# A convolution, a router and a grouped MLP on one core: the band matrix by predicated copies, zero matmuls ahead of the convolution, half batches fetched on two queues, logits in one group

## The chip, the cores and the metric

The kernel runs on one core of a Trainium2 chip. The metric is the time of one execution on the device in microseconds. One further execution was profiled; its trace gives the start and the length of every instruction, what it waited for, and the packets of the DMA engines.

## The reference

`x` is [8, 3584, 192]. A causal convolution of seven taps runs along the sequence, with softmaxed taps for each of eight heads of 24 columns; a linear router gives each of the 28,672 resulting rows to one of eight experts with a capacity of 3,584 each, best score first; each expert is an MLP 192 → 1024 → 192.

```python
w = exp(weight - max); w = w / (sum(w) + 1e-9)            # [8 heads, 7 taps]
out = einsum('hk,bskhg->bshg', w, windows of x, 7 long)   # "attn", [28672, 192]
logits = attn @ w_gate                                    # [28672, 8]
# all (token, expert) pairs in falling order of logit: a token takes the expert
# if it has none yet and the expert holds fewer than 3584
out[mask_e] = relu(attn[mask_e] @ w1[e]) @ w2[e]
```

## The kernel before

**Half batches.** The sequence is worked off in 16 half batches of 1,792 rows. Half batch i is tile X(i), [118, 16, 192] in f32: 16 windows of 112 rows on partitions 6 to 117, and the six rows ahead of each window (the halo) on partitions 0 to 5. Four such tiles take turns. X(i) comes by three transfers, halo, windows 0 to 7 ("first half") and windows 8 to 15 ("second half"). SyncE's queue (SP) issues the first two, ScalarE's queue (ACT) the third; of X(0) SP issues all. The halo of an even half batch has one window of zeros, which GpSimd (POOL) writes.

**Convolution.** `conv(i)` runs one f32 matmul for each head h against TH[:, h], a banded matrix of 118 rows that holds the seven taps on diagonals (`cv<-X,TH`; a trace shows two instructions for an f32 matmul, so 16 for a half batch). ScalarE copies the eight results into tile `a`, then issues the store of `a` to `attn` in DRAM. Four PSUM banks let TensorE run four heads ahead of these copies. Between heads `mid(h)` is called, which puts other work into the same stream.

**Band matrix.** `toeplitz` softmaxes the taps (`wb`) on VectorE and ScalarE, then builds TH head by head out of seven masks MK of 112 columns: VectorE does six heads, ScalarE and GpSimd two.

**Logits.** For half batch i-1 VectorE transposes `a` in 32x32 blocks (`aT`, four instructions), for half batch i-2 TensorE multiplies by the gate matrix `GF` (named `c_mu` in the trace; `pl<-aT,c_mu`, 24 matmuls of 32 output rows in f32, 48 instructions), ScalarE evacuates them, and one transpose (`pt`) puts them into the table LT. The list `left` in `moe_kernel` holds these pieces and `mid` takes one for each head.

**Routing and MLP.** From half batch 6 on, steps of the router (`bg` matmuls, `m_x`, `sl`, `oa`) are mixed in by a planner (`Pace`, `Meter`, `Steps.hook`) that adds up estimated engine times while the program is written, and takes no time at run time. After half batch 15 the MLP follows (`ph`, `hh`, `hl`, `y`), 56 tiles of 512 rows, with gathers and scatters by GpSimd.

**Transfers and their counters.** The built program gives all transfers of SP and ACT eight completion counters in turn (DMAHW0 to DMAHW7). A transfer that takes a counter waits until the transfer that had it before has landed, on the engine that issues it. An engine's instructions start in order, so what stands behind such a wait on ScalarE, the copies out of PSUM too, waits as well.

Of the kernel before, what the change touches and what calls it, by code (L numbers as in the profile page):

```python
# [28 lines left out]
class Meter:  # L29
# [5 lines left out]
    def __getattr__(self, op):  # L35
# [4 lines left out]
        def call(*a, **k):  # L40
# [4 lines left out]
            if self.name == "pe":  # L45
# [3 lines left out]
                p.pe += max(d + 0.0025, 0.027 if bf else 0.107)  # L49
# [64 lines left out]
def build(ctx, tc, nc, x, weight, wg, attn, LT, wk):  # L114
# [10 lines left out]
    pmi = cst.tile([128, 128], I32, name="pmi")  # L125
    P.iota(pmi, pattern=[[-1, 128]], base=0, channel_multiplier=1)
# [3 lines left out]
    P.memset(TH[:, :, W:128], 0.0)  # L130
    MK = cst.tile([128, 7, W], BF, name="MK")
    for j in range(7):
        V.tensor_scalar(MK[:, j], D0[:, 0:W], float(j), None, op0=OP.is_equal)
    wm = cst.tile([128, 8], F32, name="wm")

    def toeplitz():
# [3 lines left out]
        load(1)  # L140
# [4 lines left out]

        tk = cst.tile([128, 2, W], F32, name="tk")
        for h in (1, 5):
            A.activation(TH[:, h, 0:W], MK[:, 0], AF.Copy, scale=wb[:, h, 0:1])
            for j in range(1, 7):
                A.activation(tk[:, j % 2], MK[:, j], AF.Copy, scale=wb[:, h, j:j + 1])  # L150
                P.tensor_tensor(TH[:, h, 0:W], TH[:, h, 0:W], tk[:, j % 2], op=OP.add)
        for hs in ((0, 2), (3, 4), (6, 7)):
            for j in range(7):
                for h in hs:
                    t = TH[:, h, 0:W]
                    if j == 0:
                        V.tensor_scalar(t, MK[:, 0], wb[:, h, 0:1], None, op0=OP.mult)
                    else:
                        V.scalar_tensor_tensor(t, MK[:, j], wb[:, h, j:j + 1], t, op0=OP.mult, op1=OP.add)


    wgr = cst.tile([128, 6, 8], F32, name="wgr")
    GF = wk.tile([128, 6, 32], F32, name="c_mu")
    pm = wk.tile([128, 1], F32, name="pm")

    def gate_ops():
        for pb in range(4):
            nc.sync.dma_start(wgr[32 * pb:32 * pb + 32], wg.rearrange("(c f) e -> f c e", f=32))
        P.memset(GF, 0.0)
        for pb in range(4):  # L170
            q = slice(32 * pb, 32 * pb + 32)
            P.tensor_copy(GF[q, :, 8 * pb:8 * pb + 8], wgr[q])

        pi = cst.tile([128, 1], I32, name="pi")
        P.iota(pi, pattern=[[0, 1]], base=0, channel_multiplier=1)
        V.tensor_scalar(pi, pi, 24, None, op0=OP.bitwise_and)
        V.tensor_scalar(pm, pi, 24.0, -1.0, op0=OP.is_equal, op1=OP.mult)
# [4 lines left out]
    def load(i):  # L182
        t = X[i] = k.xp[i % 4].tile([118, 16, D], F32, name="X")
        b, hf = divmod(i, 2)
        o = x.offset + (b * 3584 + hf * 1792) * D
        if hf == 0:
            P.memset(t[0:6, 0], 0.0)
            nc.sync.dma_start(t[0:6, 1:16], bass.AP(tensor=x.tensor, offset=o + (W - 6) * D,
                                                    ap=[[D, 6], [W * D, 15], [1, D]]))
        else:  # L190
            nc.sync.dma_start(t[0:6], bass.AP(tensor=x.tensor, offset=o - 6 * D, ap=[[D, 6], [W * D, 16], [1, D]]))
        for eng, w in ((nc.sync, 0), (A if i else nc.sync, 8)):
# [46 lines left out]
    k.toeplitz, k.gate_ops = toeplitz, gate_ops  # L239
# [1180 lines left out]
def moe_kernel(ctx, tc, x, weight, wg, w1, w2, out):  # L1420
# [6 lines left out]
    with ExitStack() as cw:  # L1427
# [57 lines left out]
        def tail():  # L1485

            for i in (14, 15):
                for u in range(3):
                    gate(i, u)
                    yield PEA if u == 2 else None  # L1490
                end(i)
# [43 lines left out]
        def gate(i, u):  # L1535
            for f in range(2 * u, 2 * u + 2):
# [11 lines left out]

        k.load(0)
        k.toeplitz()  # L1550
        k.gate_ops()
        k.load(2)
        r.consts()
        for i in range(NHB):
            if i + 3 < NHB:
# [106 lines left out]
```

## Time and profile before

| | |
|---|---|
| median of three runs (lowest, highest) | 1268.86 us (1267.01, 1270.75) |
| the profiled execution: time, span of its instructions | 1268.0 us, 1266.2 us |
| TensorE, VectorE, ScalarE, GpSimd busy | 1222.0, 999.6, 551.2, 510.1 us |
| packets of the DMA engines | 193.02 MB |

The span runs from the first instruction to the last. The 1.8 us between it and the time of the same execution lie outside what the trace shows. Busy time of TensorE counts pipelined matmuls from issue to end, so that rows of matmuls overlap.

### The profile page before, as it was taken

Reading aid. Unit: us, or ns where it says so; the run is one execution under the profiler, and the core shown is the slowest. Engines: PE = TensorE matmul, PEld = TensorE weight load, DVE = VectorE, ACT = ScalarE, POOL = GpSimd, SP = SyncE. Lnnn points to the kernel's source line nnn. Section 1 sums busy time; section 2 is a strip of 40 time slices with the busy share of each in tenths; the row PEclk is TensorE's granted clock in tenths of the full one; section 3 lists DMA queues with packets and bytes.
Section 4 is the critical chain, followed back from the end, with each engine's and each line's share of the span. In section 5 each row is a group of like instructions: output and inputs, shape, how many; then the busy total and the mean of one; then the engine's idle time right before and its main releaser. Section 6 shows DMA issues by size and latency. Waiting matters only on the chain.

```text
span 1266.2 us, 21792 instructions
## 1 busy us (share of the span) xinstructions
PE 1222.0 (97%) x7839; PEld 1049.9 (83%) x7839; DVE 999.6 (79%) x2245; ACT 551.2 (44%) x1220; POOL 510.1 (40%) x504
## 2 busy tenths in 40 slices
PE   5889979999999999999999999999999999999997
PEld 2445558899889888887889999999999999999997
DVE  7398669999999989988857777777777777777772
ACT  4544645565544543643433333333333333333332
POOL 3000435364444443533244444444444444444422
PEclk9999989999999999999999999999999999999999
DMA  9999897999533343423653513242314132231100
GB/s 236 347 334 297 271 328 257 294 316 319 194 103 112 122 152 94 152 93 125 161 126 105 205 41 100 94 155 62 129 48 147 46 102 97 85 105 47 45 26 28
DMA packets 100579, 193.02 MB, mean 152 GB/s; under 512 B 19232, under 2 KB 64752, under 8 KB 96240
## 3 DMA queue, kind: packets, MB, share of 16 engines
q1 hardware_dynamic: 57856, 115.15, 28.1%
q0 software_dynamic: 21504, 44.07, 11.7%
q10 hardware_dynamic: 21104, 32.34, 7.8%
q8 instruction: 63, 1.03, 0.3%
q14 instruction: 52, 0.43, 0.1%
HBM read 116.02 MB, written 75.50 MB: 151 GB/s over the span
## 4 chain that ended last, share of the span: by engine, by line
PE 83%; DVE 7%; DMA 5%; issue 1%; POOL 1%; ACT 1%; SPq 1%; POOLq 0%; ACTq 0%; DVEq 0%
PE ph L55 38%; PE y L55 37%; PE cv L55 3%; PE bg L55 3%; DMA X<-in_x_dram 1%; PE px L55 1%; DVE X L55 1%; DMA raw<-in_moe_w_dram 1%; DVE hl L55 1%; DVE oa L55 1%; DVE aT L55 1%; DMA wgr<-in_moe_w_gate_dram 1%; PE pl L55 1%; DMA X<-otab 1%; POOL xg L1262 0%
## 5 line engine op out<-in xcount | busy, mean ns | idle before, releaser
L55 PE MATMUL y<-w,hh 128*128 128x384 f32 x1792 | 539.3, 356 | 0.0
L55 ACT ACTIVATE hh<-ph 128x512 fp32r<-128x512 f32 x448 | 268.1, 598 | 494.2 <-PE ph L55 493.9
L55 PE MATMUL y<-w,hl 128*128 128x192 f32 x1792 | 448.9, 251 | 0.0
L55 DVE SCALAR_TENSOR_TENSOR hl<-ph,hh 128x512 fp32r<-128x512 f32 x448 | 308.1, 688 | 140.6 <-ACT hh L55 136.6
L55 PE MATMUL ph<-xa,w 128*128 128x512 f32 x1344 | 395.7, 402 | 3.9 <-DVE hl L55 3.9
L55 PEld LDWEIGHTS y<-w,hl 128*128 128x128 f32 x1792 | 341.0, 190 | 15.1
L55 PEld LDWEIGHTS y<-w,hh 128*128 128x128 f32 x1792 | 336.4, 188 | 19.1 <-issue 2.3
L1337 POOL DMA_INDIRECT out_dram<-yo,ib x128 | 127.9, 999 | 288.4 <-DVE yo L55 278.6
L55 PEld LDWEIGHTS ph<-xa,w 128*128 128x128 f32 x1344 | 218.7, 189 | 24.6 <-DVE hl L55 5.2
L1337 POOL DMA_INDIRECT out_dram<-yo,ia x96 | 112.2, 1168 | 262.3 <-DVE yo L55 230.0
L55 DVE STREAM_TRANSPOSE xs<-xg 32x256 f32<-32x256 f32 x496 | 182.9, 369 | 8.5
L55 PE MATMUL ph<-xd,w 128*128 128x512 f32 x448 | 177.3, 396 | 1.5 <-DVE xd L55 1.5
L55 PE MATMUL ph<-xd,dl 128*128 128x512 f32 x448 | 174.5, 390 | 0.0
L1262 POOL DMA_INDIRECT xg<-attn,jb x128 | 137.8, 1076 | 40.9 <-issue 40.9
L1262 POOL DMA_INDIRECT xg<-attn,ja x96 | 110.2, 1147 | 32.1 <-issue 26.7
L55 ACT ACTIVATE yt<-y 128x192 f32<-128x192 f32 x224 | 73.6, 328 | 102.6 <-PE y L55 99.5
L55 PE MATMUL cv<-X,TH 118*128 118x384 f32 x256 | 99.6, 515 | 18.9 <-DVE TH L55 12.5
L55 DVE TENSOR_TENSOR yo<-y,yt 128x192 f32<-128x192 f32 x224 | 79.4, 354 | 40.8 <-ACT yt L55 38.1
L55 PEld LDWEIGHTS ph<-xd,w 128*128 128x128 f32 x448 | 84.2, 188 | 21.2 <-DVE xd L55 2.0
L55 PEld LDWEIGHTS ph<-xd,dl 128*128 128x128 f32 x448 | 84.3, 188 | 19.7
L55 PEld LDWEIGHTS cv<-X,TH 118*128 118x128 f32 x256 | 44.6, 194 | 51.8 <-issue 13.0
L55 ACT ACTIVATE a<-cv 128x384 f32<-128x384 f32 x128 | 59.7, 492 | 53.3 <-PE cv L55 32.0
(237 smaller groups left out, 900.4 us busy)
## 6 DMA issues: line engine op xcount, KB each, us to landing
w<-kw SPq DMA_DIRECT2D x16, 1536.0 KB
w<-kv SPq DMA_DIRECT2D x16, 1536.0 KB
attn<-a ACTq DMA_DIRECT2D x16, 1344.0 KB
kw<-w SPq DMA_DIRECT2D x48, 256.0 KB
kv<-w SPq DMA_DIRECT2D x32, 384.0 KB
X<-in_x_dram SPq DMA_DIRECT2D x17, 672.0 KB
X<-in_x_dram ACTq DMA_DIRECT2D x15, 672.0 KB
raw<-in_moe_w_dram SPq DMA_DIRECT2D x32, 192.0 KB
```

The source lines that it names most:

```text
L55: return f(*a, **k)
L1262: self.nc.gpsimd.indirect_dma_start(out=t[:, b], out_offset=None, in_=self.attn[0:rows], in_offset=bass.IndirectOffsetOnAxis(ap=idx[b], ax ...
L1337: st = self.nc.gpsimd.indirect_dma_start(out=self.out, out_offset=bass.IndirectOffsetOnAxis(ap=idx, axis=0), in_=o, in_offset=None, bounds ...
```

## The change

- TH comes from a narrow band C of 38 columns: a mask MK of [128, 7, 38] compared at once, seven predicated copies that write one tap each for all eight heads, and four copies of 32 partitions into TH, two on VectorE and two on ScalarE.
- 28 bf16 matmuls of a zero tile run ahead of the first convolution (`warm`).
- The gate matrix is fetched once, not four times, and VectorE places it.
- `prep` separates the zeros of the halo from `load`; `load` issues its first part (halo and first half) on SP and its second part on ACT, separately. X(0) is split over both queues too. The second half of X(i+3) is issued behind head 3 of half batch i, no longer ahead of head 0.
- The 24 logit matmuls of a half batch stand together behind head 3.
- The planner's estimate for matmuls with 32 output rows goes down.

```diff
-    D0 = cst.tile([128, 128], BF, name="D0")
-    V.tensor_copy(D0, pmi)
...
+    zb = cst.tile([128, 512], BF, name="zb")
+    V.memset(zb, 0.0)
+    BW = 38
+    pmi = cst.tile([128, 7, BW], I32, name="pmi")
+    P.iota(pmi, pattern=[[-1, 7], [-1, BW]], base=6, channel_multiplier=1)
...
+    V.tensor_scalar(MK, pmi, pf, None, op0=OP.is_equal)
...
+    def warm(n):
+        ps = k.bank("pt")
+        for _ in range(n):
+            PE.matmul(ps, zb[:, 0:128], zb, start=True, stop=True)
...
-        for h in (1, 5):
-            A.activation(TH[:, h, 0:W], MK[:, 0], AF.Copy, scale=wb[:, h, 0:1])
...
+        for j in range(7):
+            V.copy_predicated(C, MK[:, j, None, :].to_broadcast([128, 8, BW]), wb[:, :, j, None].to_broadcast([128, 8, BW]))
+        for a in (0, 3, 1, 2):
+            lo = 32 * a - 6
+            c0, c1 = max(lo, 0), min(32 * a + 32, W)
+            o, i = TH[32 * a:32 * a + 32, :, c0:c1], C[32 * a:32 * a + 32, :, c0 - lo:c1 - lo]
+            if a % 3:
+                V.tensor_copy(o, i)
+            else:
+                A.activation(o, i, AF.Copy)
...
-        for eng, w in ((nc.sync, 0), (A if i else nc.sync, 8)):
+        for p in parts:
+            eng, w = ((nc.sync, 0), (A, 8))[p]
...
-        def gate(i, u):
-            for f in range(2 * u, 2 * u + 2):
+        def gate(i):
+            for f in range(6):
                 k.logits(i, f)
...
+        k.warm(28)
+        for i in range(4):
+            k.prep(i)
         k.load(0)
+        k.load(1)
+        k.gate_load()
+        k.load(2, (0,))
+        k.load(3, (0,))
         k.toeplitz()
+        k.load(2, (1,))
         k.gate_ops()
-        k.load(2)
...
             def mid(h):
+                if h == (3 if i else 7) and i < NHB - 3:
+                    k.load(i + 3, (1,))
...
-                            left.append(partial(gate, i - 2, u) if u < 3 else partial(end, i - 2))
+                            left.append((lambda: None) if u % 2 == 0 else partial(gate if u == 1 else end, i - 2))
```

ScalarE's stream from the first convolution's end to the third's start, before. X_180, X_188, X_278, X_312 and X_352 are X(0) to X(4); a_316, a_357 and a_392 are the results of half batches 0, 1 and 2; `[waits ...]` names the counters and engines waited for.

```order
L193 DMA X_278<-in_x_dram 112x8x192
L193 DMA X_312<-in_x_dram 112x8x192 [waits DMAHW4_49]
...
L204 DMA attn_62<-a_316 112x4x768 [waits DMAHW7_49,Activation_49]
L193 DMA X_352<-in_x_dram 112x8x192 [waits DMAHW3_49,DMAHW2_49,DMAHW1_49]
L55 ACTIVATE a_357<-cv_358 128x16x24 [waits PE_49]
...
L204 DMA attn_62<-a_357 112x4x768 [waits DMAHW5_49,Activation_49]
L193 DMA X_388<-in_x_dram 112x8x192 [waits DMAHW7_49,DMAHW6_49]
L55 ACTIVATE a_392<-cv_393 128x16x24 [waits PE_49]
```

The same engine now, from its first instruction to half batch 2. X_211, X_213, X_214, X_216, X_320 and X_356 are X(0) to X(5); a_283, a_324 and a_359 belong to half batches 0, 1 and 2.

```order
L208 DMA X_211<-in_x_dram 112x8x192
L208 DMA X_213<-in_x_dram 112x8x192
L55 ACT_TABLE_LOAD
...
L208 DMA X_214<-in_x_dram 112x8x192 [waits DMAHW0_49]
...
L208 DMA X_216<-in_x_dram 112x8x192 [waits DMAHW3_49]
L55 ACTIVATE a_283<-cv_315 128x16x24 [waits PE_49]
L219 DMA attn_62<-a_283 112x4x768 [waits DMAHW5_49,Activation_49]
...
L208 DMA X_320<-in_x_dram 112x8x192 [waits DMAHW2_49,DMAHW4_49,DMAHW0_49,Pool_49]
L55 ACTIVATE a_324<-cv_338 128x16x24 [waits PE_49]
...
L55 ACTIVATE a_359<-cv_368 128x16x24 [waits PE_49]
L208 DMA X_356<-in_x_dram 112x8x192 [waits DMAHW6_49,DMAHW5_49]
```

The second halves of X(0) and X(1) now stand ahead of everything on ScalarE, those of X(4) and X(5) between copies inside half batches 1 and 2. DMAHW0 is held by the second half of X(2) when X(4) asks for it, and DMAHW5 by the store of half batch 0 when X(5) asks for it.

SP's first rows, before (X_180, X_188 and X_278 as above):

```order
L188 DMA X_180<-in_x_dram 6x15x192
L193 DMA X_180<-in_x_dram 112x8x192 x2
L191 DMA X_188<-in_x_dram 6x16x192
L193 DMA X_188<-in_x_dram 112x8x192
L168 DMA wgr_141<-in_moe_w_gate_dram 32x6x8 [waits DMAHW0_49]
...
L168 DMA wgr_141<-in_moe_w_gate_dram 32x6x8 [waits DMAHW3_49]
L188 DMA X_278<-in_x_dram 6x15x192 [waits DMAHW5_49]
```

And now:

```order
L202 DMA X_211<-in_x_dram 6x15x192
L208 DMA X_211<-in_x_dram 112x8x192
L205 DMA X_213<-in_x_dram 6x16x192
L208 DMA X_213<-in_x_dram 112x8x192
L176 DMA wgr_143<-in_moe_w_gate_dram 32x6x8
L202 DMA X_214<-in_x_dram 6x15x192 [waits DMAHW1_49]
L208 DMA X_214<-in_x_dram 112x8x192 [waits DMAHW2_49]
```

X(2) now waits for small or early transfers, where it waited behind the four gate transfers and for X(1).

TensorE in half batches 3 and 4, before (`pt` ends the half batch two earlier; counts are matmuls):

```order
L55 MATMUL pt<-ident,L 128x128
L55 MATMUL cv<-X,TH 128x384 x2
L55 MATMUL pl<-aT,c_mu 32x128 x8
L55 MATMUL cv<-X,TH 128x384 x2
L55 MATMUL pl<-aT,c_mu 32x128 x8
L55 MATMUL cv<-X,TH 128x384 x2
L55 MATMUL pl<-aT,c_mu 32x128 x8
L55 MATMUL cv<-X,TH 128x384 x2
L55 MATMUL pt<-ident,L 128x128
```

And now:

```order
L55 MATMUL pt<-ident,L 128x128
L55 MATMUL cv<-X,TH 128x384 x4
L55 MATMUL pl<-aT,c_mu 32x128 x24
L55 MATMUL cv<-X,TH 128x384 x4
L55 MATMUL pt<-ident,L 128x128
```

The matmuls are the same; three groups of logits between heads became one.

## Rows read from the trace of the kernel before

**Rows 1.** Stretches: length, busy (count) per engine, TensorE's granted clock, DMA share, GB/s.

```profile
0.00:10.00 10.00, 0.00 (x0) 0.00 (x0) 6.24 (x25) 4.65 (x12) 3.41 (x14) 1.00 0.75 171
10.00:20.00 10.00, 7.48 (x15) 3.78 (x16) 9.08 (x33) 4.92 (x12) 4.78 (x11) 1.00 1.13 231
...
27.00:33.00 6.00, 4.16 (x40) 2.11 (x40) 2.78 (x4) 0.00 (x0) 0.00 (x0) 1.00 1.05 373
...
45.00:62.50 17.50, 17.50 (x153) 9.24 (x152) 7.86 (x10) 9.96 (x27) 0.25 (x1) 1.00 1.05 337
...
70.00:100.00 30.00, 26.61 (x224) 13.74 (x222) 25.99 (x67) 14.61 (x38) 0.49 (x2) 1.00 1.04 335
...
131.70:157.50 25.80, 25.80 (x250) 14.71 (x249) 14.23 (x33) 17.23 (x42) 13.25 (x13) 1.00 0.80 253
157.50:190.00 32.50, 25.00 (x192) 18.46 (x191) 19.77 (x32) 14.17 (x33) 10.41 (x11) 0.84 0.97 324
```

**Rows 2.** The first 26 us in order of time: start, length, what.

```profile
4.45 0.21 DVE L55 TENSOR_REDUCE wm<-wb 128x8 f32<-128x56 f32 x1 [2.13 <-DMA wb<-in_weight_dram]
...
5.92 0.22 DVE L55 TENSOR_TENSOR wb<-wb,wm 128x56 f32<-128x56 f32 x1
...
11.61 6.45 PE L55 MATMUL cv<-X,TH 118*128 118x384 f32 x12 [11.61 <-DVE TH L55]
...
16.05 3.02 DVE L55 SCALAR_TENSOR_TENSOR TH<-MK,wb,TH 128x112 f32<-128x112 bf16 x12
...
18.98 6.69 PE L55 MATMUL cv<-X,TH 118*128 118x384 f32 x20 [0.91 <-DVE TH L55]
```

**Rows 3.** TensorE's matmuls in order of time, from 25 us on.

```profile
28.17 1.53 PE L55 MATMUL cv<-X,TH 118*128 118x384 f32 x4 [2.50 <-DMA X<-in_x_dram]
...
43.78 1.56 PE L55 MATMUL cv<-X,TH 118*128 118x384 f32 x4 [1.90 <-ACT a L55]
...
47.35 1.45 PE L55 MATMUL cv<-X,TH 118*128 118x384 f32 x4
48.73 0.64 PE L55 MATMUL pl<-aT,c_mu 128*32 128x128 f32 x16
49.31 1.56 PE L55 MATMUL cv<-X,TH 118*128 118x384 f32 x4
50.80 0.64 PE L55 MATMUL pl<-aT,c_mu 128*32 128x128 f32 x16
...
54.94 1.45 PE L55 MATMUL cv<-X,TH 118*128 118x384 f32 x4
...
62.53 1.45 PE L55 MATMUL cv<-X,TH 118*128 118x384 f32 x4
...
131.68 1.45 PE L55 MATMUL cv<-X,TH 118*128 118x384 f32 x4
```

**Rows 4.** TensorE's weight loads of half batch 0.

```profile
12.38 0.34 PEld L55 LDWEIGHTS cv<-X,TH 118*128 118x128 f32 x1 [0.30 <-POOL TH L151]
13.02 0.34 PEld L55 LDWEIGHTS cv<-X,TH 118*128 118x128 f32 x1 [0.30 <-issue]
```

**Rows 5.** What ScalarE waited for up to 70 us: total, times, longest.

```profile
ACT a L55 <- DMA attn<-a: 7.5, 1, 7.5
```

**Rows 6.** Transfers: queue, count, size of one.

```profile
attn<-a ACTq DMA_DIRECT2D x16, 1344.0 KB
...
X<-in_x_dram ACTq DMA_DIRECT2D x15, 672.0 KB
```

**Rows 7.** The chain that ended last, up to 200 us: start, length, what.

```profile
25.05 17.70 DMA X<-in_x_dram
...
166.87 7.25 DMA raw<-in_moe_w_dram
...
199.18 1.18 PE ph L55 x5
```

**Rows 8.** The page's costliest groups: a VectorE pass over 512 columns.

```profile
L55 DVE SCALAR_TENSOR_TENSOR hl<-ph,hh 128x512 fp32r<-128x512 f32 x448 | 308.1, 688 | 140.6 <-ACT hh L55 136.6
```

More of the change, by code (lines that the diff above doesn't have):

```diff
@@ L124, in build @@
     nc.sync.dma_start(wb, bass.AP(tensor=weight.tensor, offset=weight.offset, ap=[[0, 128], [7, 8], [1, 7]]))
-    pmi = cst.tile([128, 128], I32, name="pmi")
-    P.iota(pmi, pattern=[[-1, 128]], base=0, channel_multiplier=1)
-    D0 = cst.tile([128, 128], BF, name="D0")
-    V.tensor_copy(D0, pmi)
-    TH = cst.tile([128, 8, 128], F32, name="TH")
[L130 to L133, printed above, removed]
+    zb = cst.tile([128, 512], BF, name="zb")
[3 more added lines that the diff above has]
+    P.iota(pmi, pattern=[[-1, 7], [-1, BW]], base=6, channel_multiplier=1)
+    pi = cst.tile([128, 1], I32, name="pi")
+    P.iota(pi, pattern=[[0, 1]], base=0, channel_multiplier=1)
+    C = cst.tile([128, 8, BW], F32, name="C")
+    P.memset(C, 0.0)
+    TH = cst.tile([128, 8, 128], F32, name="TH")
+    P.memset(TH, 0.0)
+    pq = cst.tile([128, 1], I32, name="pq")
+    V.tensor_scalar(pq, pi, 96, None, op0=OP.bitwise_and)
+    pf = cst.tile([128, 1], F32, name="bandf")
+    V.tensor_copy(pf, pq)
+    MK = cst.tile([128, 7, BW], I32, name="MK")
+    V.tensor_scalar(MK, pmi, pf, None, op0=OP.is_equal)
     wm = cst.tile([128, 8], F32, name="wm")
+    def warm(n):
+        ps = k.bank("pt")
+        for _ in range(n):
+            PE.matmul(ps, zb[:, 0:128], zb, start=True, stop=True)
     def toeplitz():
@@ L139, in toeplitz @@
         A.activation(wb, wb, AF.Exp)
-        load(1)
         V.tensor_reduce(wm, wb, axis=AX.X, op=OP.add)
@@ L144, in toeplitz, with gate_load @@
         V.tensor_tensor(wb, wb, wm[:, :, None].to_broadcast([128, 8, 7]), op=OP.mult)
-        tk = cst.tile([128, 2, W], F32, name="tk")
-        for h in (1, 5):
-            A.activation(TH[:, h, 0:W], MK[:, 0], AF.Copy, scale=wb[:, h, 0:1])
[L149 to L162, printed above, removed]
+        for j in range(7):
[8 more added lines that the diff above has]
+                A.activation(o, i, AF.Copy)
+    wgr = cst.tile([32, 6, 8], F32, name="wgr")
     GF = wk.tile([128, 6, 32], F32, name="c_mu")
     pm = wk.tile([128, 1], F32, name="pm")
+    def gate_load():
+        nc.sync.dma_start(wgr, wg.rearrange("(c f) e -> f c e", f=32))
     def gate_ops():
-        for pb in range(4):
-            nc.sync.dma_start(wgr[32 * pb:32 * pb + 32], wg.rearrange("(c f) e -> f c e", f=32))
         P.memset(GF, 0.0)
@@ L171, in gate_ops @@
             q = slice(32 * pb, 32 * pb + 32)
-            P.tensor_copy(GF[q, :, 8 * pb:8 * pb + 8], wgr[q])
-        pi = cst.tile([128, 1], I32, name="pi")
-        P.iota(pi, pattern=[[0, 1]], base=0, channel_multiplier=1)
+            V.tensor_copy(GF[q, :, 8 * pb:8 * pb + 8], wgr)
         V.tensor_scalar(pi, pi, 24, None, op0=OP.bitwise_and)
@@ L1487, in tail @@
             for i in (14, 15):
-                for u in range(3):
-                    gate(i, u)
-                    yield PEA if u == 2 else None
+                gate(i)
+                yield PEA
                 end(i)
```

27 lines of the change are left out of this document (16 added, 11 removed).

## The prediction

> **What bounds the kernel now.** I read the stretches first, then the first 26 us in order of time, then TensorE's matmuls and the chain that ended last.
>
> The stretches split the run in three. From 45 to 62.5 us TensorE is busy for all 17.50 us, from 131.7 to 157.5 for all 25.80 [rows 1]. From 70 to 100 it is busy 26.61 of 30 while VectorE has 25.99: the router's steps share the path. Up to 45 us TensorE is not the limit. Nothing runs on it for 11.61 us, until the band matrix is there; then it runs the heads of half batch 0 as VectorE finishes them, to 19.1 us (16.05 + 3.02) [rows 2]. Half batch 2 starts at 28.17 after a wait of 2.50 for X, and half batch 3 is broken at 43.78 by 1.90 behind ScalarE [rows 3]. ScalarE itself was held: once 7.5 us for the store of half batch 0 [rows 5], and before 43.78 by the transfer of X that began at 25.05 and took 17.70 [rows 7]. The DMA share is 0.75 in the first ten microseconds and above 1 after that; but the rate is 231 GB/s between 10 and 20 us, when hardly anything but x moves, and 373 between 27 and 33, when the first stores run beside the loads [rows 1]. So the front is set by the band matrix first, and then by transfers that are many, late and slow.
>
> From 47.35 the half batches run without a wait: 54.94 - 47.35 and 62.53 - 54.94 are 7.59 us each [rows 3]. What the change gives must be seen at half batch 6, which starts at 62.53; all behind it is TensorE's and the router's, whose matmuls do not change.
>
> **The change, part by part.**
>
> *Band matrix.* The softmax stands unchanged and ends at 6.14 (5.92 + 0.22). The six heads on VectorE took until 19.1. In their place come seven predicated copies of 304 columns. The trace has none. Twelve fused passes over 112 columns took 3.02 us, 0.25 each [rows 2]; one over 512 takes 0.688 [rows 8]; on the line between them 304 columns are 0.46, and seven 3.2 us. The bounds are 1.8 (all at 0.25) and 4.8 (all at 0.688); I take 3.2 since the width lies between. Two copies of as many columns for each of two engines side by side add 0.9. TH is complete at 6.14 + 3.2 + 0.9, about 10.3 (9 to 12), all heads at once.
>
> *Zero matmuls.* 512 columns cost 1.18 / 5 = 0.24 us in the MLP [rows 7]; 28 are 6.6 us there. The engine has been idle before, and half batch 0 shows what that means: its weight loads stood 13.02 - 12.38 = 0.64 apart [rows 4], while later matmuls stand (6.69 - 1.56) / 16 = 0.32 apart [rows 2, 3]; that is 1.2 against 2.4 GHz, though the stretch's granted clock reads 1.00. So 28 take 6.6 us at the upper level and 13.2 at the lower. From 1.3 us (the zero tile) they end between 7.9 and 14.5; I take 9.5, a mix as in half batch 0, hidden behind the band matrix. At the late end half batch 0 starts 4 us later; the wait in half batch 2 below then covers most of that.
>
> *X(0) and X(1).* X(0) is 1.45 MB (twice 672 KB and the halo [rows 6]); the first ten microseconds moved 1.71 MB [rows 1], so it is in at about 9. With its halves on two queues, and X(1)'s second half ahead of X(0)'s first, it may be in between 8.5 and 11. I start half batch 0 at 10.5. Its 16 matmuls at 0.32 end at 15.7, those of half batch 1 at 20.9. The second half of X(4) stands behind head 3 of half batch 1 on ScalarE and asks for the counter of X(2)'s second half, in at about 19; four banks cover all but some 0.6: half batch 2 starts at 21.5.
>
> *The first wait that takes the place of one.* Behind head 3 of half batch 2 the second half of X(5) asks for the counter that the first store holds. By then X(0) to X(3), that store and one half of X(4) have to move: 5.8 + 1.4 + 0.8 = 8.0 MB. From the rows, 1.7 MB are through at 10 us and 3.3 at 17 at 231 GB/s; from 17 on stores run beside loads, and at 337 to 373 GB/s [rows 1] the other 4.7 take 12.6 to 13.9 us. So ScalarE stands from about 23.5 to 30, where it stood 7.5 us before at a later place [rows 5]. Queued behind it are five copies of half batch 2; TensorE runs four heads ahead and then waits. Half batch 3 starts at 31.5, and 4 to 6 follow at 7.3 to 7.6 us (next part): half batch 6 at 53.5 instead of 62.53, **9.0 us** gained. With the front's rate as it was until 27 us the store lands at 33, and the gain is 5.5. With no wait at all half batch 6 starts at 21 + 4 × 7.2 = 49.8, and the gain is 12.7.
>
> *Logits in one group.* A group costs more than its matmuls: four convolution instructions are 1.28 at 0.32, but 50.80 - 49.31 = 1.49 when a group stands on either side, so 0.2 for a group. Two groups fewer are 0.4 us: 7.59 becomes 7.2. For half batches 2 to 5 transfers take that away: a half batch moves 1.45 + 1.38 MB, 7.6 us at 373 GB/s. For 6 to 12 it would be 2.8 if TensorE were alone there; VectorE has 25.99 of 30 us, so I take half, **1.5 us** (0 to 2.8). In 13 to 15, where TensorE is always busy, three half batches of logits stand in three groups instead of nine: 6 × 0.2, **1.0** after rounding down.
>
> *Gate matrix and zeros of the halo* move off the path; their cover is the 20 us before half batch 2's logits. If that cover were gone they would cost their four 32-row copies, some 2 us.
>
> *Start of the MLP.* From 157.5 to 190 us TensorE is busy 25.00 of 32.50 and the granted clock is 0.84 [rows 1]; the chain shows weights that took 7.25 us to land [rows 7]. These transfers hang on the last half batches by order, and the DMA share ahead of them is 0.80, so I move them along and take 0, with -2 to +2.
>
> The sum is 9.0 + 1.5 + 1.0 = 11.5: a span of 1254.7, a time of 1256.5 by the profiled execution, whose 1268.0 lies 0.9 below the median. I say 1257.
>
> **A rule against it.** That x moves at 231 GB/s at a share of 1.13 says that the DMA engines, not the issue, limit the front. The Trainium skill (DMA: Bandwidth & Descriptors, § Issuing engines are not separate DMA queues) says the same in general: transfers started on several engines run on the same 16 DMA engines, and several issuers save only the time to issue. By it the two queues bring nothing of themselves; that is the first rival.
>
> **Rivals.**
>
> 1. *Transfers set the front anyway.* If loads stay at 231 GB/s beside the stores' start, the gain is the 5.5 above, and the shorter half batches are eaten by transfers too: 6.5 in all, 1262. For it speaks the share above 1 from 10 us on; against it the 373 GB/s as soon as stores join.
> 2. *No wait in the front.* TensorE runs from 10.5 us without a stop: 12.7 + 2.8 + 1.2 = 16.7, 1252. It needs 2.83 MB in 7.2 us, 393 GB/s, more than any stretch of the rows.
> 3. *Slower: a wait behind head 3 in every half batch.* The load now stands inside the copies of its half batch; if its counter comes late each time, TensorE stops each time. Two such stops are in the rows of before, the longer 1.90 [rows 3]. In eleven half batches (2 to 12) that is 21 us against 11.5: 1278. It decides from about 1.05 us a half batch. Against it: the counter asked for is that of the half batch after the next one's own X, two periods old, and four banks cover.
> 4. *Given back at the MLP.* If weights, not the convolution, set its start, some 10 us become waits after 157.5: 1266. Against it: share 0.80 before it.
>
> **How the numbers follow.** Chances: the forecast 0.58, rival 1 0.13, rival 2 0.15, rival 3 0.06, rival 4 0.08. A difference under 0.3% (3.8 us) can't be told from none. Faster: 0.58 + 0.15 and most of rival 1, 0.85; same 0.09; slower 0.06. The range goes from rival 2 with its late terms, 1250, to the bound of 5.5 less 2 at the MLP, 1264.5; the forecast's own is 1252 to 1261.
>
> **What would show it.** TH complete and half batch 0 running at 0.32 from 10 to 11 us; half batch 2 held on ScalarE by the first store until about 30; half batch 6 at 53 to 54; one `pl` group and about 7.2 us where no router step stands. It is wrong if half batch 6 starts after 58, if ScalarE waits for X behind head 3 in many half batches, or if TensorE's idle time after the convolution grows by more than 3 us.

## The result, and the profile after

The changed kernel took 1273.16 us (median of nine runs, 1270.70 to 1275.05) and the kernel before 1268.86: a ratio of 1.003, 95% interval 1.0015 to 1.0044. It is slower by 0.3%, where 1257 was forecast and 1250 to 1264.5 was the range. The profiled execution took 1271.89 us with a span of 1270.1, 3.9 longer than before.

The stretches of the changed kernel, with the columns of [rows 1]:

```profile
0.00:10.00 10.00, 8.65 (x28) 3.26 (x28) 4.54 (x14) 1.53 (x2) 4.13 (x20) 1.00 0.62 143
10.00:20.00 10.00, 4.29 (x7) 2.42 (x8) 2.31 (x6) 1.82 (x5) 0.00 (x0) 0.66 1.11 227
27.00:33.00 6.00, 5.32 (x61) 3.18 (x59) 3.81 (x5) 1.47 (x3) 0.00 (x0) 1.00 1.08 318
45.00:62.50 17.50, 17.50 (x178) 10.89 (x171) 7.87 (x10) 10.07 (x28) 0.25 (x1) 1.00 1.07 336
70.00:100.00 30.00, 25.29 (x206) 14.50 (x205) 25.26 (x67) 14.26 (x39) 0.49 (x2) 0.94 1.04 360
100.00:131.70 31.70, 29.41 (x294) 19.57 (x294) 25.86 (x47) 12.34 (x32) 1.22 (x2) 0.84 0.88 272
131.70:157.50 25.80, 25.41 (x271) 16.85 (x269) 16.87 (x35) 17.37 (x43) 9.77 (x10) 1.00 0.81 266
157.50:190.00 32.50, 22.70 (x173) 16.54 (x174) 18.47 (x30) 14.60 (x32) 13.93 (x14) 0.84 0.90 304
```

Before, the granted clock was 1.00 in the first seven of these stretches: six stand in [rows 1], and this is the stretch from 100 to 131.7 us in the kernel before:

```profile
100.00:131.70 31.70, 29.61 (x311) 19.02 (x308) 28.69 (x51) 14.24 (x35) 1.20 (x2) 1.00 1.00 299
```

Now it is 0.66 from 10 to 20 us, 0.94 from 70 to 100 and 0.84 from 100 to 131.7. The first 24 us of the changed kernel in order of time:

```profile
1.20 8.65 PE L55 MATMUL pt<-zb 128*128 128x512 bf16 x28 [1.20 <-DVE zb L55]
...
6.31 0.21 DVE L55 TENSOR_REDUCE wm<-wb 128x8 f32<-128x56 f32 x1 [3.66 <-DMA wb<-in_weight_dram]
...
7.77 0.22 DVE L55 TENSOR_TENSOR wb<-wb,wm 128x56 f32<-128x56 f32 x1
8.10 3.70 DVE L55 COPY_PREDICATED C<-MK,wb 128x304 f32<-128x304 int32 x7
...
12.32 0.35 ACT L55 ACTIVATE TH<-C 32x176 f32<-32x176 f32 x1
...
15.71 8.72 PE L55 MATMUL cv<-X,TH 118*128 118x384 f32 x20 [5.86 <-DMA X<-in_x_dram]
```

The new band matrix does what it says: seven copies in 3.70 us, TH complete at 12.67, all heads at once. But the taps land 1.9 us later than in [rows 2], and TensorE stands idle for 5.86 us between the zero matmuls and half batch 0. For the last 3.0 of them (15.71 - 12.67) TH is complete and only X(0) is missing. The chain that ended last shows what took the time:

```profile
1.61 13.96 DMA X<-in_x_dram
...
15.71 7.44 PE cv L55 x16
...
23.69 14.26 DMA attn<-a
...
164.45 8.85 DMA raw<-in_moe_w_dram
...
1262.28 0.66 POOL out_dram L1352
```

X(0)'s first half was under way for 13.96 us, and the store of half batch 0 for 14.26, until 37.95. ScalarE stood behind head 3 of half batch 2 for the end of the latter. The wait list has it (3.8 us, where [rows 5] had 7.5):

```profile
ACT L L55 <- DMA attn<-a: 3.8, 1, 3.8
```

TensorE's matmuls, which answer to [rows 3]:

```profile
39.33 0.91 PE L55 MATMUL cv<-X,TH 118*128 118x384 f32 x2 [3.28 <-ACT a L55]
...
48.80 2.74 PE L55 MATMUL cv<-X,TH 118*128 118x384 f32 x8
...
55.72 2.74 PE L55 MATMUL cv<-X,TH 118*128 118x384 f32 x8
...
62.64 2.74 PE L55 MATMUL cv<-X,TH 118*128 118x384 f32 x8
...
114.11 0.67 PE L55 MATMUL bg<-X,oa 128*128 128x16 bf16 x8 [0.79 <-DVE oa L55]
...
122.09 4.50 PE L55 MATMUL cv<-X,TH 118*128 118x384 f32 x8
```

A half batch without waits takes 6.92 us (55.72 - 48.80), where it took 7.59; and half batch 6 starts at 62.64 where it started at 62.53. From there on time is lost: the same eight matmuls take 4.50 us in half batch 12, and the first gather of the MLP goes out at 147.9 instead of 144.1.

### The profile page after: what moved, and what is told of

The parts are those of the page before. It is cut to its first block, busy times and chain, and to the rows that moved or that the text cites. A ratio compares the mean times of both kernels' runs of the same rounds, so it can differ in the third digit from the quotient of the medians.

```text
span 1270.1 us, 21788 instructions
## 1 busy us (share of the span) xinstructions
PE 1228.7 (97%) x7875; PEld 1059.3 (83%) x7875; DVE 986.6 (78%) x2196; ACT 546.4 (43%) x1208; POOL 500.4 (39%) x489
## 3 DMA queue, kind: packets, MB, share of 16 engines
q0 software_dynamic: 21504, 44.07, 11.6%
## 4 chain that ended last, share of the span: by engine, by line
PE 84%; DVE 8%; DMA 5%; issue 2%; ACT 1%; SPq 0%; POOL 0%; POOLq 0%; ACTq 0%; DVEq 0%
PE ph L55 38%; PE y L55 37%; PE cv L55 4%; PE bg L55 2%; DVE X L55 2%; PE px L55 1%; DVE aT L55 1%; DMA attn<-a 1%; DMA X<-in_x_dram 1%; DMA raw<-in_moe_w_dram 1%; DVE hl L55 1%; DVE oa L55 1%; DMA kw<-w 1%; DMA xg<-attn,ja 1%; PE pl L55 1%
## 5 line engine op out<-in xcount | busy, mean ns | idle before, releaser
L55 DVE STREAM_TRANSPOSE xs<-xg 32x256 f32<-32x256 f32 x480 | 177.0, 369 | 8.2
L1277 POOL DMA_INDIRECT xg<-attn,ja x96 | 106.6, 1111 | 29.7 <-issue 26.7
L55 PEld LDWEIGHTS cv<-X,TH 118*128 118x128 f32 x256 | 49.4, 207 | 49.7 <-issue 18.3
L55 ACT ACTIVATE a<-cv 128x384 f32<-128x384 f32 x128 | 59.8, 492 | 38.8 <-PE cv L55 27.6
```

The source lines that it names most:

```text
L55: return f(*a, **k)
L1277: self.nc.gpsimd.indirect_dma_start(out=t[:, b], out_offset=None, in_=self.attn[0:rows], in_offset=bass.IndirectOffsetOnAxis(ap=idx[b], ax ...
```

## The experiments

Runs 1 to 4, 5 to 8, 9 to 12, 13 to 16 and 17 to 18 shared a chip each, with runs of the kernel before on it, which took 1269.6 to 1276.9 us (medians) there; so ratios are compared, not times. The changed kernel itself was timed on one chip only. Most of the program can be read from five marks of a trace, all in us: the start of half batches (hb) 0 and 6, the first gather behind half batch 6 (the router's pace), the last copy into LT (the MLP may start), and the time from the last `yt<-y` to the end of the span. The stretch between the last LT and the last `yt<-y` is not among them; it took 1072.9 to 1085.9 us. Each row has the marks of one trace, and the ratio of many executions.

| run | hb 0 | hb 6 | gather behind hb 6 | last LT | end | ratio (95%) |
|---|---|---|---|---|---|---|
| before | 11.6 | 62.5 | 81.6 | 184.6 | 7.2 | 1 |
| changed | 15.7 | 62.6 | 85.3 | 187.2 | 9.1 | 1.003 (1.0015, 1.0044) |
| 1 front alone | 15.6 | 62.7 | 81.5 | 185.9 | 9.1 | 1.002 (1.0007, 1.0034) |
| 2 logits alone | 11.8 | 61.5 | 85.6 | 186.8 | 7.0 | 1.0004 (0.9989, 1.0019) |
| 3 X(0) first | 11.5 | 57.1 | 84.0 | 182.3 | 8.9 | 0.9998 (0.9985, 1.0012) |
| 4 X(5) late | 15.5 | 63.2 | 83.1 | 187.8 | 9.0 | 1.0034 (1.0021, 1.0047) |
| 5 clock kept | 15.9 | 63.1 | 80.5 | 187.6 | 8.9 | 1.0049 (1.0036, 1.0063) |
| 6 GpSimd padded | 15.3 | 62.3 | 85.3 | 190.2 | 8.1 | 1.0014 (1.0001, 1.0026) |
| 7 all X on SyncE | 11.5 | 61.3 | 83.3 | 188.2 | 9.1 | 1.0022 (1.0011, 1.0034) |
| 8 = 3 + 5 + 6 | 11.5 | 58.6 | 83.9 | 182.8 | 8.3 | 0.9986 (0.9972, 1.0000) |
| 9 X(0) first, three groups, padded | 11.4 | 58.5 | 81.5 | 179.0 | 7.4 | 0.9950 (0.9937, 0.9962) |
| 10 split on VectorE | 15.5 | 62.3 | 83.6 | 186.3 | 9.2 | 0.9989 (0.9975, 1.0002) |
| 11 = 3 + 10, padded | 11.5 | 55.4 | 83.5 | 180.5 | 7.1 | 0.9949 (0.9935, 0.9963) |
| 12 = 9 + 10 | 11.7 | 58.5 | 80.0 | 180.6 | 7.0 | 0.9969 (0.9950, 0.9987) |
| 13 X(1) late | 12.7 | 60.0 | 83.0 | 183.2 | 9.5 | 1.0004 (0.9988, 1.0021) |
| 14 both padded | 15.5 | 63.0 | 83.0 | 184.8 | 7.4 | 0.9997 (0.9980, 1.0014) |
| 15 = 9 without zeros | 11.5 | 58.0 | 81.5 | 178.2 | 7.3 | 0.9949 (0.9931, 0.9967) |
| 16 before again | 12.2 | 66.4 | 81.5 | 187.7 | 7.0 | 0.9993 (0.9977, 1.0009) |
| 17 = 15, load ahead of head 0 | 11.5 | 62.9 | 81.6 | 186.0 | 7.1 | 1.0000 (0.9985, 1.0015) |
| 18 = 15, grouped, old estimate | 11.0 | 57.7 | 85.9 | 185.5 | 7.3 | 1.0017 (0.9997, 1.0037) |

"Padded" stands for one-element memsets that bring the number of instructions near that of the kernel before: 26 to 36 on GpSimd and up to 36 on VectorE, not the same in every run (run 18 has ten more on VectorE than run 15).

**Runs 1 and 2, the two halves of the change.** Run 1 undoes the grouping and the estimate in the changed kernel; run 2 makes only these two in the kernel before.

```diff
-            left.append((lambda: None) if u % 2 == 0 else partial(gate if u == 1 else end, i - 2))
+            left.append(partial(gate, i - 2, u) if u < 3 else partial(end, i - 2))
```

> The front of the change alone: new band matrix, zero matmuls, order of loads; the logits stand in three groups and the planner's estimate is the old one. Theory 1 (the grouped logits are what costs: VectorE sets half batches 6 to 12, TensorE idles in longer pieces there and its granted clock falls to 0.84 between 100 and 131.7 us): half batch 6 starts about 1.5 us later than with the grouping (64 instead of 62.64), the granted clock from 70 to 131.7 us is back at 1.00, the gathers go out as far behind half batch 6 as before, and the time is 1267 to 1270, no slower than the kernel before. Theory 2 (the grouping saves the 2.5 us that the prediction gave it, and the front loses more than that): 1274 to 1277.

> The logits alone: the kernel before with 24 logit matmuls in one group and the planner's new estimate. Theory 1: half batch 6 starts 1 to 1.5 us earlier than before (61.2), but by half batch 12 that is lost, with a granted clock under 0.95 between 70 and 131.7 us, and the time is 1269 to 1273. Theory 2: 1265.5 to 1267, with 7.2 us or less for a half batch all the way.

The gather came out as theory 1 has it: it stands 81.5 us behind half batch 6 with three groups and 85.6 with one, whatever the front is. Half batch 6 starts at 62.7 in run 1, not at 64. The times did not follow theory 1: neither half carries the loss alone, and 1.002 for run 1 lies above its range. So a third thing had to be looked for, and the last column shows it: 9.1 us at the end wherever the front is new, 7.0 where it is not.

**Run 3, X(0) ahead of X(1).**

```diff
-            eng, w = ((nc.sync, 0), (A, 8))[p]
+            eng, w = ((nc.sync, 0), (A if i else nc.sync, 8))[p]
...
         A.activation(wb, wb, AF.Exp)
+        load(1, (1,))
...
-        k.load(1)
+        k.load(1, (0,))
```

> The changed kernel, but both halves of X(0) go out on SyncE ahead of all of X(1), and the second half of X(1) on ScalarE behind the exponential, as before. If the split of X(0) over two queues with X(1) beside it is what makes it late (13.96 us from issue to landing): half batch 0 starts at 11 to 12.5 instead of 15.71. Then two outcomes. If the store of half batch 0 (14.26 us from issue to landing) sets half batch 3 by its place in time, half batches 3 and 6 start 3 to 4 us earlier, 36.5 and 59, and the time is 1269 to 1270. If the bytes of all transfers set it, half batch 3 stays at 39 to 41 and the time at 1272 to 1274.

Half batch 0 starts at 11.5 (TH, not X, is the last thing it waits for), half batch 3 at 32.0, half batch 6 at 57.1. The first outcome holds, by more than expected.

**Run 13, X(1)'s second half alone moved.** X(0) stays split; `load(1, (1,))` stands behind the exponential as in run 3.

> The changed kernel with one transfer moved: the second half of X(1) goes out on ScalarE behind the exponential and not ahead of everything; X(0) stays split over both queues. If X(0) was late because X(1) went beside it: half batch 0 starts at 11 to 12.5 us, half batch 6 at 57 to 58, as with X(0) whole on SyncE, and the ratio is 0.9995 to 1.001. If the split itself made it late (ScalarE's queue taking the DMA engines from SyncE's, where the taps and the first half stand): half batch 0 starts at 13.5 or later.

12.7 and 60.0, so neither case came whole: the transfer that went beside X(0) made most of the delay (15.7 to 12.7), the split the rest (12.7 to 11.5 in run 3). What the queues moved in the first 9 us (packets, MB, share of 16 engines), in the changed kernel, where q10 is ScalarE's queue and q1 SyncE's:

```profile
q10 hardware_dynamic: 1330, 1.01, 48.1%
q1 hardware_dynamic: 327, 0.16, 8.8%
```

in run 13:

```profile
q1 hardware_dynamic: 823, 0.54, 28.8%
q10 hardware_dynamic: 912, 0.69, 28.8%
```

and in run 3:

```profile
q1 hardware_dynamic: 1933, 1.38, 67.3%
```

and in the kernel before:

```profile
q1 hardware_dynamic: 1997, 1.43, 71.2%
```

The taps and X(0)'s first half stand on SyncE's queue, which got 0.16 of 1.17 MB. The two queues together also moved less in these 9 us (1.17 and 1.23 MB) than SyncE's queue alone (1.38 and 1.43); no run shows why.

**Runs 4 and 7, the waits of ScalarE.** Run 4 issues the second half of X(5) behind head 7 of half batch 2, run 7 all halves of X on SyncE.

```diff
-                if h == (3 if i else 7) and i < NHB - 3:
+                if h == (7 if i in (0, 2) else 3) and i < NHB - 3:
```

> The changed kernel, but the second half of X(5) stands behind head 7 of half batch 2 instead of head 3. If the wait for the counter of the first store, with five copies behind it, sets half batch 3 (40.19 now): TensorE runs through half batch 2 and half batch 3 starts 3 to 5 us earlier (35.5 to 37.5), half batch 6 at 58 to 60, and the time is 1268 to 1270. If X(3) or the transfers as a whole set it, half batch 3 starts at 39 or later and the time stays at 1272 to 1274.

> The changed kernel with all halves of X on SyncE's queue, in the order X(0), X(1), gate matrix, X(2), X(3) at the start, and later the second half at its place behind head 3, but on SyncE: ScalarE issues only stores and never waits for the counter of a load. If X(0) behind X(1) is what made the front late, half batch 0 starts at 11 to 12.5 us and half batch 6 at 57 us or earlier. If the waits behind head 3 on ScalarE cost as well, beyond X(0), half batch 3 to 6 run without a break behind ScalarE and half batch 6 starts at 52 to 55. If transfers as a whole set it, it starts at 57 or later, as with X(0) first alone (57.1). The time is then 1 to 6 us below the changed kernel, of which the start of the MLP may take a part back.

In run 4 half batch 3 starts at 36.2 instead of 40.2, as the wait demands, but half batch 6 at 63.2. TensorE waits for no X on the way; it waits behind ScalarE's copies, 1.73, 0.42, 1.28 and 1.46 us. ScalarE in turn was busy issuing transfers, which mostly took it 0.32 us each and here much longer:

```profile
38.95 4.77 ACTq L208 DMA_DIRECT2D X<-in_x_dram  x1
...
46.38 3.06 ACTq L219 DMA_DIRECT2D attn<-a  x1
```

So what the wait's end gave was lost again behind ScalarE. In run 7 TensorE waits four times for X, 9.3 us in all, and half batch 6 starts at 61.3 although half batch 0 started at 11.5: with one queue for all loads, X is late as well.

**Runs 15 and 17, what the front is worth.** Run 9 is the front with X(0) first, three groups and 26 memsets each on GpSimd and VectorE; run 15 leaves its zero matmuls out; run 17 puts the load back ahead of head 0.

```diff
-        k.warm(28)
```

```diff
-                k.load(i + 3, (0,))
+                k.load(i + 3)
+            if i == 0:
+                k.load(3, (1,))
...
-                if h == (3 if i else 7) and i < NHB - 3:
-                    k.load(i + 3, (1,))
```

> The front with X(0) ahead of X(1), as in the third run, but logits in three groups and the old estimate; GpSimd and VectorE get 26 one-element memsets each, so that both execute as many instructions as in the kernel before to within a few. If the grouped logits are only a loss (clock at half speed in half batches 11 and 12): half batch 6 starts at 58.5 (57.1 and three times 0.4 to 0.7 for the groups), the clock stays at 1.00 to the end of the convolution, half batch 12 stands 57.2 us behind half batch 6 as before, the first gather goes out at 140, the end behind the last copy of y is 7.0 us, and the ratio is 0.995 to 0.9975. If what the convolution gains is given back at the MLP's start whatever the logits do, the ratio is 0.998 to 1.0, as with three repairs together (0.9986).

> The run with X(0) first and logits in three groups, without the 28 zero matmuls. If they do what the prediction took them for (nothing of themselves but a faster start of half batch 0): half batch 0 starts at 11.4 as before and takes 0 to 1.5 us longer, half batch 6 starts within 1 us of 58.5, and the ratio stays at 0.994 to 0.9965. If they matter: half batch 6 at 60 or later and a ratio over 0.997.

> The run without zero matmuls (X(0) first, logits in three groups, memsets for the code's place), with the second half of X(i+3) issued on ScalarE ahead of head 0 of half batch i, as in the kernel before, and not behind head 3. What is left of the change is the band matrix, the gate matrix and the zeros of the halo. If the gain of 0.5% of that run (0.9949) comes from the band matrix and the order of the first loads: half batch 6 at 57 to 60 and a ratio of 0.994 to 0.9975. If the place behind head 3 brings it: half batch 6 at 61 or later and a ratio of 0.9985 or more.

Run 9 gives 0.9950, 0.5% faster than the kernel before, and run 15 the same: the zeros do nothing for the time (half batch 0 takes 6.93 us with them and 8.31 without, and half batch 2 starts at 24.3 and 24.9). The place behind head 3 brings all that the times can tell: with the load ahead of head 0 the ratio is 1.0000 and half batch 6 starts 5.0 us later. Runs 15 and 17 were timed on different chips, each against the kernel before. What ScalarE then waits for transfers up to 62.5 us, in run 17:

```profile
ACT a L55 <- DMA X<-in_x_dram: 9.8, 3, 4.7
ACT a L55 <- DMA attn<-a: 5.8, 1, 5.8
```

In run 15 its list names no transfer, but ScalarE waits there too, twice, behind head 3 of half batches 3 and 4. Its copies had ended at 37.17 and 44.97, the counters asked for came free at 39.61 and 48.44, and the loads went out right after; the list puts the idle time down to matmuls that had long ended:

```profile
39.68 0.32 ACTq L209 DMA_DIRECT2D X<-in_x_dram  x1
40.04 0.87 ACT L55 ACTIVATE a<-cv 128x384 f32<-128x384 f32 x2 [2.87 <-PE cv L55]
...
48.51 0.32 ACTq L209 DMA_DIRECT2D X<-in_x_dram  x1
48.87 0.87 ACT L55 ACTIVATE a<-cv 128x384 f32<-128x384 f32 x2 [3.90 <-PE cv L55]
```

In run 15 five copies of the half batch stand behind such a wait, in run 17 all eight, and the difference is what reaches TensorE. Up to 62.5 us it waits for copies in run 17:

```profile
PE cv L55 <- ACT a L55: 6.4, 3, 3.0
```

and in run 15:

```profile
PE cv L55 <- ACT a L55: 1.9, 2, 1.1
```

**Runs 5 and 18, the grouped logits.** Run 5 puts zero matmuls at two places where TensorE waits for VectorE (one is shown, its last line shortened); run 18 groups the logits in run 15 with the old estimate.

```diff
+                if h == 0 and z < 40 and per == 8:
+                    for _ in range(8):
+                        nc.nc.tensor.matmul(ps[:, 16 * (z % 32):16 * (z % 32) + 128], self.zb[:, 0:128], ...)
```

> The changed kernel with zero matmuls of 128 columns put where TensorE waits for VectorE: twelve ahead of each of the last two count matmuls of the threshold, eight ahead of each of the first five groups of oa matmuls. They add about 4 us of work to TensorE where it idles, and change no result. Theory 1 (the fall of the granted clock to half speed from 115.4 to 125.6 us, which the grouped logits bring by leaving TensorE idle in longer pieces, is what half batches 12 to 14 lose): the clock stays at 1.00 from 100 to 131.7 us, half batch 12 starts 2 to 3 us earlier behind half batch 6 (57 us instead of 59.45), the first gather goes out 2.5 to 3.5 us earlier, and the time is 1 to 3 us below that of the changed kernel, a ratio to the kernel before of 1.001 to 1.002. Theory 2 (VectorE's chain sets it, the clock costs nothing): half batch 12 at 59 or later behind half batch 6, ratio 1.003 or more.

> The run without zero matmuls with the logits in one group, but the planner's old estimate for them. If the idle pieces of TensorE and its fall to half speed come from the grouping itself: the first gather stands 83 to 85.5 us behind half batch 6 (81.5 with three groups), the clock falls between half batches 9 and 12, and the ratio is 0.0005 to 0.003 above that of three groups. If they come from the new estimate, which lets the planner put steps of the router elsewhere: 81.5 or less, no fall, and the ratio is that of three groups (0.9949) or 0.001 below it.

In the changed kernel VectorE is full from 112 to 114 us and TensorE has 1.11 of 2 us; then the clock is at its lower level, 1.2 GHz, until 125.6 (two-microsecond stretches, columns as above):

```profile
110.00:112.00 2.00, 2.00 (x49) 1.33 (x48) 2.00 (x4) 0.61 (x2) 0.00 (x0) 1.00 0.88 215
112.00:114.00 2.00, 1.11 (x21) 0.75 (x10) 2.00 (x5) 0.81 (x3) 0.00 (x0) 1.00 1.10 251
114.00:116.00 2.00, 1.89 (x12) 1.32 (x13) 2.00 (x4) 0.44 (x1) 0.00 (x0) 0.85 1.06 412
116.00:118.00 2.00, 2.00 (x19) 1.52 (x18) 2.00 (x5) 0.29 (x2) 0.00 (x0) 0.50 1.01 371
```

The stretch from 100 to 131.7 us in run 5:

```profile
100.00:131.70 31.70, 31.09 (x361) 22.54 (x362) 28.22 (x50) 14.46 (x37) 1.22 (x2) 1.00 0.94 293
```

and in run 1, with three groups:

```profile
100.00:131.70 31.70, 29.61 (x317) 18.86 (x307) 28.85 (x51) 13.71 (x35) 1.20 (x2) 1.00 0.99 301
```

With the clock kept the gather stands 80.5 us behind half batch 6, 4.8 us less, and below every trace with one group in which the clock fell (83.0 to 85.9): that part of theory 1 holds. But the size of the gather's delay does not follow the length of the fall. In run 13 the clock was low for 3.4 us between half batch 6 and the gather, and the gather stands at 83.0; in runs 4 and 14 it was low for 10.2 us, and the gather stands at 83.1 and 83.0. Theory 1's time does not hold either: last LT at 187.6, ratio 1.0049. By the marks, what the router won was lost between the gather and the last LT (44.1 us); the changed kernel takes 39.3 there, and runs 6 and 14, which only add memsets to it, 42.6 and 38.8.

Run 18 met neither of its cases. The convolution is done earlier still (half batch 15 at 137.6), and from half batch 6 on the clock holds until half batch 13. Yet the gather stands 85.9 us behind half batch 6 and the ratio is 0.0068 above that of run 15: there the convolution runs ahead of the router's steps. By the marks grouping delays the gather with either estimate, in part by the clock with the new one and by the order with the old one; the order is argued from these marks alone. In the times the loss is clear with the old estimate only. With the new one run 3 lies 0.0048 above run 9, which the end explains in part (8.9 and 7.4 us), but run 1 is hardly faster than the changed kernel, and run 11 (below) is as fast as run 9.

**Runs 6 and 14, the end.** One-element memsets in half batch 2, 26 on GpSimd, in run 14 also 36 on VectorE.

```diff
+                for _ in range(26):
+                    P.memset(junk, 0.0)
+                for _ in range(36):
+                    nc.nc.vector.memset(junkv, 0.0)
```

> The changed kernel with 26 one-element memsets more on GpSimd, which then executes as many instructions before the branch at the end (1245) as with the logits alone (1245) and nearly as in the kernel before (1244). From the last copy of y to the end of the span were 7.2 us in the kernel before and 6.9 with the logits alone, but 9.1 in the changed kernel: its GpSimd starts 3.8 us after the branch instead of 0.5. If that is a matter of where the code behind the branch lies: GpSimd goes on 0.5 us behind the branch, the end is 7.0 us, and the time is 2 us below the changed kernel, a ratio of 1.0015. If it hangs on something else (the last scatter, the semaphores), the end stays at 9.1 us and the ratio at 1.003.

> The changed kernel with 26 one-element memsets on GpSimd and 36 on VectorE, nothing else. If the end of the program is a matter of where the code behind the branch lies, and both engines count: 7.0 to 7.3 us from the last copy of y to the end instead of 9.1, the rest as in the changed kernel (half batch 6 at 62.6, the first gather at 147.9), and a ratio 0.0015 lower, 1.0010 to 1.0020. If the end costs nothing in the time as measured: 1.003.

The end fell to 8.1 and to 7.4 us, the ratio to 1.0014 and 0.9997. The latter is more than the end explains: 0.0033 of 1270 us are 4.2 us, and the end fell by 1.8. What the rest is stays open; it may be the chip. The last row of the chain of the changed kernel (above) stands at 1262.28 in a span of 1270.1; that of the kernel before, in a span of 1266.2:

```profile
1260.33 0.66 POOL out_dram L1337
```

So 1270.1 - 1262.28 - 0.66 = 7.2 us follow the last row where 1266.2 - 1260.33 - 0.66 = 5.2 did. In the trace's list of events GpSimd goes on 0.48 us behind the branch that skips the general path in the kernel before and in every run in which it has executed 1244 or 1245 instructions by then, and 3.3 to 4.2 us behind it in every run with 1210 to 1220. The fetches of code that follow (queue q14, 8 KB each) are six in the changed kernel, five in the kernel before and in run 14. That it is the place of the code is argued from these; that it follows the instructions added on GpSimd is shown.

**Runs 8, 10, 11 and 12, repairs together and the MLP's start.** Runs 10 to 12 compute the low halves of the first weights on VectorE.

```diff
-                    ff.wsplit(-1, P)
+                    ff.wsplit(-1, V)
```

> Three repairs together: X(0) ahead of all of X(1) on SyncE, the zero matmuls that keep the clock, the 26 memsets. If the three add up: X(0) first was 1.0032 lower than the changed kernel's ratio (0.9998 against 1.003), 2 to 3 us for the clock and 2 us for the end make a ratio of 0.996 to 0.997, 1264 to 1265 where the kernel before takes 1268.9. If the start of the MLP, whose weights then set it, takes the clock's part back: 0.998.

> The changed kernel, but in half batches 14 and 15 the low halves of the first weights (w, dl) are computed by VectorE and not by GpSimd. On GpSimd three of the four stand behind eight gathers of 1.3 us, and SyncE, whose queue is in order, waits with kd<-dl from 149 to 160.3 us, with 22 transfers of weights behind it. Theory G (the MLP's start hangs on this chain of weights): the transfers go out some 10 us earlier, TensorE's wait of 4.85 us for ScalarE's copy of L at 182.9 goes, the last transpose of logits ends 4 us or more earlier than 187.2, and the time is 2 to 5 us below the changed kernel, ratio 0.999 to 1.0015. Theory H (the transfers there run at the rate of the DMA engines, and starting earlier only puts them beside the gathers and the last stores): the last transpose stays within 2 us of 187.2 and the ratio at 1.002 to 1.004.

> X(0) first, grouped logits, weights split on VectorE, and memsets on GpSimd (36) and VectorE (26) for the place of the code behind the branch. Theory G: the 8.8 us by which the convolution ended earlier with X(0) first reach the MLP; last transpose of logits at 176 to 179 instead of 182.3, ratio 0.993 to 0.996. Theory H: 181 to 183, ratio 0.998 to 0.9995.

> The same with logits in three groups and the old estimate. If grouping costs by the clock: 1 to 3 us faster than the same with grouped logits, and the fastest of all, ratio 0.991 to 0.995. If grouping costs nothing net: equal to it within 0.15%.

Run 8 lies a little above its second case (0.9986 for 0.998). Its zero matmuls did not keep the clock, which fell from 124.5 to 127.9 us, and the gather stands at 83.9. With the split the gather comes earlier in run 12 than in run 9 (80.0 against 81.5) and in run 10 than in the changed kernel (83.6 against 85.3, where run 14 has 83.0 without it), the last LT hardly or not at all (180.6 against 179.0, 186.3 against 187.2). By the marks theory H fits, that an earlier start only puts the weights beside other transfers. By the times it does not: run 10's 0.9989 and run 11's 0.9949 lie below what theory H allows, with intervals clear of the changed kernel's 1.003 and of run 8's 0.9986. So what the split gains stays open. Of runs 9 and 12 three groups without the split are the faster; of runs 11 and 12 grouped logits are, against expectation. Both differences lie within the intervals.

**Run 16, the kernel before once more.**

> The kernel before once more, for a second trace of it: half batch 6 within 1 us of 62.5, the first gather 81.6 us behind that, the last transpose of logits 40 to 42 us behind the gather, 7.2 us from the last copy of y to the end. What of these differs by more than 1 us from the first trace is scatter between executions, and no difference between kernels of that size is explained.

Half batch 6 starts at 66.4, not 62.5: half batch 3 took 14.11 us where it took 9.56, and in it TensorE waited 3.50 us behind ScalarE, which had waited 6.2 us for a transfer of X. The gather and the end agree within 0.2 us; from the gather to the last LT it took 39.7 us instead of 40.5. The front of the kernel before scatters by 4 us; so the 62.6 of the changed kernel is no proof of "no gain", but all seven traces with its front lie at 62.3 to 63.2, and the seven with X(0) whole first and the second halves behind head 3 on ScalarE at 55.4 to 58.6.

Behind the front the changed kernel scatters too. Runs 6 and 14 only add memsets to it, yet the gather stands at 85.3 and 83.0 and the last LT at 190.2 and 184.8. With three groups and no split the gather stands at 81.5 or 81.6 in all six traces. So one group without zero matmuls delays it by 1.4 us at least, and of the 3.7 in the trace of the changed kernel up to 2.3 may be scatter.

## Why the prediction was wrong, point by point

- **X(0) and X(1): this step failed.** "it may be in between 8.5 and 11. I start half batch 0 at 10.5": it was in at 15.57. I counted bytes over both queues (1.71 MB in ten microseconds [rows 1]) and not which queue they come from: 1.01 of the first 1.17 MB were second halves on ScalarE's queue. The rate fell as well, to 1.43 MB in ten microseconds. Runs 3 and 13 undo it, and half batch 6 starts 5.5 and 2.6 us earlier; by the times run 3 gives 0.0032 back (1.003 to 0.9998), 4 us. So this step cost 5.5 of the 9.0 us forecast for the front; in the changed kernel half batch 6 started 0.1 us later than before (62.64 for 62.53).
- **The rule against it** (Trainium skill, DMA: Bandwidth & Descriptors, § Issuing engines are not separate DMA queues): two issuers share the same engines. The trace agrees, 227 GB/s between 10 and 20 us where it was 231 [rows 1]; the second queue did worse than bring nothing: what it moved was moved ahead of what was needed first.
- **Band matrix**: 3.70 us for 3.2, 12.67 for 10.3, of which 1.9 are the late taps. Right in kind.
- **Zero matmuls**: they end at 9.85 (9.5 forecast), hidden. Then TensorE idles 5.86 us, the clock falls from 13.0 to 19.8 and the weight loads of half batch 0 stand 0.64 apart again [rows 4]. Run 15: worth nothing.
- **The first wait behind head 3** was found, its place, counter and store; it ended at 37.95 instead of 30, since the store began at 23.69 and not near 16, and all queues together moved 236 GB/s from 20 to 27 us and 318 from 27 to 33, where 337 to 373 was taken from 17 us on. With X(0) in time (and both queues loading) half batch 3 starts at 31.8 to 32.6, where 31.5 was forecast. What I left out comes next: in run 15 ScalarE waits again behind head 3 of half batches 3 and 4, and issuing a transfer holds it for up to 2.73 us. Half batch 3 takes 9.0 to 11.3 us in these runs, so that half batch 6 stands at 55.4 to 58.6 and not at 53.5.
- **Logits in one group**: -1.5 and -1.0 were forecast. **This step failed too, in sign.** A half batch without waits does get shorter, to 6.92 us where 7.2 was forecast. But from 62.5 to 131.7 us every wait of TensorE is for VectorE (6.2 us before, 7.6 now); there the group takes work from between these waits, the clock falls, and the gather comes 3.7 us later in this trace, not 1.5 earlier (81.6 to 85.3).
- **Start of the MLP**: 0 (-2 to +2) was forecast; from the gather to the last LT are 39.3 us for 40.5, so 1.2 came back. In run 5 the same stretch is 4.8 us longer. What rival 4 describes, a gain of the convolution given back at the MLP, fits run 5's marks, but the scatter of this stretch (38.8 to 42.6 in runs 14 and 6) is nearly as large.
- **Not in the sum**: 1.9 us at the program's end.
- **The rivals**: rival 3 (a wait behind head 3 in every half batch, some 1.90 us each for TensorE) did not come: the changed kernel has one such wait in half batch 2, run 15 two, in half batches 3 and 4, that cost TensorE 1.06 and 0.85. Rival 1 came nearest in its mechanism, since run 4 gave back what it won, but run 9 shows that the order of transfers, not only their number, sets the front.

By the marks: 0.1 at half batch 6, +3.7 in the router, -1.2 to the last LT, -0.7 to the last `yt`, +1.9 at the end make 3.9 before rounding. Single traces scatter by up to 2.3 us up to the gather and 3.8 from there to the last LT, so these parts are rough. By the times only two parts can be told: the padding, which shortens the end (1.003 to 0.9997 in run 14, intervals that just do not touch, and more than the end alone explains), and the order of X(0). The versions that beat the kernel before clearly are run 15 (X(0) first, load behind head 3, three groups, padding, no zeros), 0.9949; run 9, the same with zeros, 0.9950 on another chip; and run 11 (X(0) first, one group, split on VectorE, padding), 0.9949.

## What to carry to other kernels

Ask of every early transfer what else is issued before it lands, on any queue: here a second queue was served at the cost of the first, and what was needed first came last. A wait behind which copies stand is worth moving behind some of these copies, but only with the transfers ahead of it in time. Where another engine sets the pace, gathering TensorE's small work into one piece takes the filler out of its waits and can cost the clock. A couple of microseconds at the end can come with the number of instructions ahead of it and have nothing to do with what was changed. And a wait list can name the wrong engine: look at what stands just ahead of the instruction that waited.

## What the runs showed of the hardware that was not expected

- Two queues did not share evenly: 1.01 MB against 0.16 in the first 9 us, with 1330 and 327 packets, where ScalarE had issued two halves of 672 KB ahead of SyncE's first; 0.69 against 0.54 where it had issued one (run 13). Together they moved 1.17 and 1.23 MB, where one queue moved 1.38 (run 3) and 1.43 (before).
- Issuing one transfer took ScalarE 4.40 us (the store of half batch 1 at 28.85) in the changed kernel and up to 5.44 in others (run 14), where most took 0.32; copies stood behind it.
- The granted clock was 0.5 for 10.2 us (115.4 to 125.6) after TensorE had waited 0.21 and 0.79 us between groups of 16-column matmuls, and did not fall in run 5, in which zero matmuls stood there.
- 26 memsets on GpSimd and 36 on VectorE in the middle of the program shortened its end by 1.8 us (9.1 to 7.4).
